# Eight block sums at the end of each up stage, on GpSimd in place of VectorE

## The chip, the cores and the metric

The kernel runs on one core of one Trainium2 chip. The metric is the device time of one execution in microseconds (us). The kernel before was timed three times: 1130.04, 1131.62 and 1132.43 us, median 1131.62 us.

Engine names are those of the profile: PE is TensorE's matmul stream and PEld its weight loads, DVE is VectorE, ACT is ScalarE, POOL is GpSimd, SP is the engine whose queue issues nearly all transfers (SPq). SBUF is the memory on the chip that all engines read, PSUM the one that PE writes its sums to.

## The reference

The reference is an attention followed by two feed-forward stages. What matters here are the two stages; in numpy, on 1792 tokens of 768 features:

```python
def _moe_ref(x, w_in, w_out):                 # d_ff = 2048
    h = np.maximum(x @ w_in, 0.0)
    return (h * h @ w_out).astype(np.float32)

def _moe2_ref(x, w_gate, w_val, w_out):       # d_ff = 1536
    g = x @ w_gate
    silu = g * (1.0 / (1.0 + np.exp(-g)))
    val = x @ w_val
    return (silu * val @ w_out).astype(np.float32)
```

Each stage is an up product (into the hidden features), an elementwise function, and a down product (back to 768 features).

## The kernel before

**Seven products for eight.** Each matrix product is cut into two by two blocks and done by a scheme with seven block products (P1 to P7) in place of eight. Its operands are blocks and sums of blocks: of the hidden result, the blocks B11, B12, B21, B22 and four differences of them, T1 = B12 - B11, T3 = B22 - B12, T2 = B22 - T1, T4 = B21 - T2. The down product reads B21, T1, B22, B11, T2, T3 and T4, in that order (`DOWN`, `DUSE`).

**Splitting for precision.** PE multiplies in a format that is shorter than fp32. Every operand is therefore split in two: a high part, made on ACT by a cast, and a low part, made on DVE by a subtraction (value minus high part). Three matmuls take the place of one: high by high, high by low, low by high. PE can't begin a step before both parts of its operands are there. For the hidden blocks the split is `cleave` (L1303 for the high part on ACT, the low part on DVE through `tt`, L1102, written to `xat` in the first stage and to `xab` in the second); for the weights it is L516 on ACT and L271 on DVE, into the five buffers `ring`.

**Loops and order.** An up stage runs over groups of 2 x 128 hidden features: eight groups in the first stage (`ph` 0), six in the second, where each has a gate and a value part. Within a group come the seven products, each for the two halves of the tokens (`tp` 0 and 1); a matmul has 448 columns. One `step` is one product for one half: nine matmuls. `after` evicts a result from PSUM, by ACT (L1105) or with an addition on DVE (L1102, `xacc<-ps,xacc`). When the blocks of a group are complete, `put` enters the T sums into a list with a due time, counted in steps, and `run_sums` issues them through `sum_of`: on DVE, two inputs and one output of 128x448 in SBUF (L1102, `xacc<-xacc`). A finished block is sent to DRAM by SP two to five steps later (`hid<-xacc`, L1059), and comes back for the down product (`dn<-hid`, L1281) with both halves side by side. Each group has eight such sums, four for each half.

The down product is `down`: seven products of `ng` steps each (eight in the first stage, six in the second), 18 matmuls a step. Step n needs the two parts of the n-th hidden block (`cleave(n, 0)` and `cleave(n, 1)`) and of the n-th weight block. The order of the instructions on each engine is fixed by the program. `cleave(n + 2, 1)` is issued in step n before `run_sums` of the same step. For the last group, the sums fall due as follows: T1 of half 0 in the last step of the up stage, between the low parts of down step 0 and of down step 1; T3 of half 0 and T1 of half 1 in down step 0; T2, T3, T2 and T4 in down step 1; the last T4 in down step 2. Block B21 of the last group isn't sent through DRAM but split straight from where it lies.

POOL works in the attention only, adding probabilities (L783), normalising (L698) and scaling the result (L848); after 274 us it has no instruction left. SP's queue takes its transfers in order: the sends of the T sums, the loads of hidden blocks and of weights stand in one line.

The diff touches one line of `sum_of` (L1073).

Of the kernel before, what the change touches and what calls it, by code (L numbers as in the profile page):

```python
# [13 lines left out]
ALU = mybir.AluOpType  # L14
# [5 lines left out]
def kernel(  # L20
# [14 lines left out]
    nc = tc.nc  # L35
# [16 lines left out]
    NF = (DFF // P, DFF2 // P)  # L52
# [19 lines left out]
    def slot(s):  # L72
        return xacc[:, s * S:(s + 1) * S]
# [931 lines left out]
    def moe():  # L1005
# [38 lines left out]
        def run_sums():  # L1044
            now = [d for d in sums_due if d[0] <= clock["n"]]
            sums_due[:] = [d for d in sums_due if d[0] > clock["n"]]
            for _, args in now:
                sum_of(*args)
# [15 lines left out]
        def drop(m, name):  # L1064
            m["left"][name] -= 1
            if not m["left"][name]:
                free.append(m[name])

        def sum_of(ph, g, tp, name):
            m = parts[ph, g, tp]  # L1070
            a, b = {"T1": ("B12", "B11"), "T3": ("B22", "B12"), "T2": ("B22", "T1"), "T4": ("B21", "T2")}[name]
            m[name] = m["B12"] if name == "T3" else take()
            tt(nc.vector, slot(m[name]), slot(m[a]), slot(m[b]), ALU.subtract)  # L1073
            for x in (a, b):
                if x != "B12":
                    drop(m, x)
# [24 lines left out]
        def tt(eng, o, a, b, op=ALU.add):  # L1101
            eng.tensor_tensor(out=o, in0=a, in1=b, op=op)  # L1102
# [43 lines left out]
        def take():  # L1146
            return free.pop(0)
# [315 lines left out]
```

## Time and profile before

| what | value |
|---|---|
| median of three timed runs | 1131.62 us |
| profiled execution, its time | 1129.42 us |
| its span, first to last instruction | 1127.6 us |
| PE busy | 1112.9 us, 99% of the span |
| DVE busy | 872.0 us, 77% |
| ACT busy | 637.1 us, 56% |
| POOL busy | 211.8 us, 19%, all of it in the first quarter |
| granted TensorE clock | full, 1.000 on average |
| up stage 1, down stage 1, up stage 2, down stage 2 | from about 251, 457, 667 and 970 us |

Times within the trace count from the first instruction. In a timeline row stand the start, the time, the engine, the line, the operation, output and inputs, how many like it follow one another, and in brackets the idle time of the engine before it with what ended that. Rows of several merged instructions give the time from the first start to the last end; instructions of DVE overlap a little at their ends, so a pair of two 0.62 us sums is listed with 1.15 us. A line can be that of a helper: L1102 is every two-input operation that goes through `tt`, so the output and the inputs tell which it is.

### The profile page before, as it was taken

The numbers are of one execution on the slowest core, as the hardware profiler recorded it, in microseconds if no ns is written. First come the engines' busy times: TensorE is split into PE (matmuls) and PEld (weight loads), VectorE is DVE, ScalarE is ACT, GpSimd is POOL, SyncE is SP. The second block draws the span as 40 slices with busy tenths as digits, with TensorE's granted clock in tenths as the row PEclk, the third lists the DMA queues.
The fourth block names the chain that finished last, engine by engine and source line by source line (L and its number), as shares of the span: only waits on it lengthen the run. The fifth ranks groups of instructions, "written<-read, shape, count | busy, mean of one in ns | idle before, by whom it ended". The sixth has DMA issues, their size and how long they took to land.

```text
span 1127.6 us, 17076 instructions
## 1 busy us (share of the span) xinstructions
PE 1112.9 (99%) x6164; PEld 946.4 (84%) x6164; DVE 872.0 (77%) x1255; ACT 637.1 (56%) x1049; POOL 211.8 (19%) x220
## 2 busy tenths in 40 slices
PE   7999999999999999999999999999999999999998
PEld 5556655559989999899999999999999999999997
DVE  7778888769897887898657788979787885875554
ACT  6887887665876676755544545443443534355332
POOL 5899899742000000000000000000000000000000
PEclk9999999999999999999999999999999999999999
DMA  6444333110798987965544402756464651874552
GB/s 166 129 115 126 99 98 82 46 35 18 238 299 273 296 288 255 346 234 184 184 130 119 127 1 79 246 165 192 142 209 141 224 173 68 309 257 125 180 164 98
DMA packets 115812, 187.76 MB, mean 167 GB/s; under 512 B 13840, under 2 KB 97040, under 8 KB 115728
## 3 DMA queue, kind: packets, MB, share of 16 engines
q1 hardware_dynamic: 115408, 186.68, 51.7%
q8 instruction: 48, 0.79, 0.3%
q14 instruction: 36, 0.29, 0.1%
q10 hardware_dynamic: 320, 0.00, 0.0%
HBM read 128.19 MB, written 58.28 MB: 165 GB/s over the span
## 4 chain that ended last, share of the span: by engine, by line
PE 89%; DMA 3%; DVE 3%; ACT 2%; issue 1%; SPq 0%; POOL 0%; DVEq 0%; ACTq 0%; POOLq 0%
PE ps L1140 41%; PE ps L1345 30%; PE s L792 6%; PE s L777 6%; PE s L748 2%; PE s L716 2%; PE s L813 2%; ACT xacc L1105 1%; DMA dn<-wkeep 1%; DVE xacc L1102 1%; PE s L757 1%; DMA raw<-in_k_dram 1%; DMA xacc<-in_moe_w_in_dram 1%; DVE mxz L751 0%; DVE conv L268 0%
## 5 line engine op out<-in xcount | busy, mean ns | idle before, releaser
L1140 PE MATMUL ps<-xb,ring 128*128 128x448 f32 x1080 | 225.6, 365 | 1.3 <-ACT xacc L1105 1.3
L1140 PEld LDWEIGHTS ps<-xb,ring 128*128 128x128 f32 x1080 | 202.8, 188 | 17.7 <-ACT xacc L1105 1.7
L1345 PE MATMUL ps<-xat,ring 128*128 128x448 f32 x1008 | 205.2, 366 | 1.3 <-DVE xat L1102 1.3
L1345 PEld LDWEIGHTS ps<-xat,ring 128*128 128x128 f32 x1008 | 189.1, 188 | 17.3 <-DVE xat L1102 2.3
L1140 PE MATMUL ps<-xat,ring 128*128 128x448 f32 x720 | 155.5, 365 | 0.0
L1345 PE MATMUL ps<-xab,ring 128*128 128x448 f32 x756 | 153.7, 365 | 0.2 <-DVE xab L1102 0.2
L1345 PEld LDWEIGHTS ps<-xab,ring 128*128 128x128 f32 x756 | 141.9, 188 | 11.9 <-DVE xab L1102 0.6
L1140 PEld LDWEIGHTS ps<-xat,ring 128*128 128x128 f32 x720 | 135.2, 188 | 10.7
L1105 ACT ACTIVATE xacc<-ps 128x448 f32<-128x448 f32 x148 | 79.0, 543 | 94.8 <-PE ps L1140 86.6
L1102 DVE TENSOR_TENSOR xacc<-ps,xacc 128x448 f32<-128x448 f32 x164 | 100.1, 620 | 34.3 <-PE ps L1140 20.7
L268 DVE SCALAR_TENSOR_TENSOR conv<-xacc,conv 128x768 int32<-128x768 int32 x124 | 119.7, 965 | 3.6
L1105 ACT ACTIVATE xacc<-xacc 128x448 f32<-128x448 f32 x148 | 85.0, 577 | 65.8 <-DVE xacc L1102 62.9
L1140 PE MATMUL ps<-xab,ring 128*128 128x448 f32 x540 | 116.2, 365 | 0.0
L751 DVE TENSOR_REDUCE mxz<-s 112x2 f32<-112x896 f32 x96 | 100.4, 1089 | 16.9 <-PE s L748 16.7
L1140 PEld LDWEIGHTS ps<-xab,ring 128*128 128x128 f32 x540 | 101.3, 188 | 8.7 <-issue 0.7
L1303 ACT CAST xat<-dn 128x896 fp32r<-128x896 f32 x55 | 51.9, 943 | 94.2 <-PE ps L1345 61.5
L271 DVE TENSOR_TENSOR ring<-conv,ring 128x384 fp32r<-128x384 f32 x127 | 70.7, 567 | 41.6 <-ACT ring L516 41.5
L779 ACT ACTIVATE p<-s 112x896 f32<-112x896 f32 x96 | 87.8, 920 | 20.8 <-PE s L777 16.1
L783 POOL TENSOR_TENSOR sg<-p 112x896 f32<-112x896 f32 x46 | 96.9, 2108 | 14.3 <-ACT p L779 14.3
L1102 DVE TENSOR_TENSOR xacc<-xacc 128x448 f32<-128x448 f32 x148 | 88.2, 618 | 1.1
L1102 DVE TENSOR_TENSOR xat<-dn,xat 128x896 fp32r<-128x896 f32 x55 | 59.9, 1088 | 34.2 <-ACT xat L1303 34.0
L1303 ACT CAST xab<-dn 128x896 fp32r<-128x896 f32 x41 | 38.7, 945 | 76.1 <-PE ps L1345 57.8
(101 smaller groups left out, 1363.9 us busy)
## 6 DMA issues: line engine op xcount, KB each, us to landing
hid<-xacc SPq DMA_DIRECT2D x192, 224.0 KB
dn<-hid SPq DMA_DIRECT2D x96, 448.0 KB
xacc<-in_moe_w_out_dram SPq DMA_DIRECT2D x28, 768.0 KB
xacc<-in_moe_w_in_dram SPq DMA_DIRECT2D x16, 768.0 KB
xacc<-in_moe_w_gate_dram SPq DMA_DIRECT2D x12, 768.0 KB
xacc<-in_moe_w_val_dram SPq DMA_DIRECT2D x12, 768.0 KB
wkeep<-conv SPq DMA_DIRECT2D x22, 384.0 KB
dn<-wkeep SPq DMA_DIRECT2D x44, 192.0 KB
```

The lines of the kernel that those rows point to most:

```text
L268: nc.vector.scalar_tensor_tensor(out=out, in0=in0, scalar=scalar, in1=out, op0=op, op1=ALU.bitwise_or)
L271: nc.vector.tensor_tensor(out=out, in0=a, in1=b, op=ALU.subtract)
L751: nc.vector.tensor_reduce(out=mxz[:, c, 0:P:D], in_=ps[:CP, :, :S], op=ALU.max, axis=AX.X)
L777: nc.tensor.matmul(ps[:CP, a, :S], lhs, rhs, start=(w == 0), stop=(w == 3))
L779: nc.scalar.activation(out=p, in_=ps[:CP, :, :S], func=AF.Exp)
L783: nc.gpsimd.tensor_tensor(out=sg, in0=p_t[pi, 2 * w], in1=p_t[pi, 2 * w + 1], op=ALU.add)
L792: nc.tensor.matmul(ps[s, :S], v_t[pi][:, a, c * D:(c + 1) * D], p[:, a, :], start=(c == 0), stop=(c == NCH - 1),)
L1102: eng.tensor_tensor(out=o, in0=a, in1=b, op=op)
L1105: nc.scalar.activation(out=slot(s), in_=src, func=func)
L1140: nc.tensor.matmul(ps, w[:, wi, kk * P:(kk + 1) * P], xk[:, xi, kk * S:(kk + 1) * S], start=bool(first and mm == 0), stop=(mm == 3 * KT - ...
L1303: nc.scalar.copy(k[:, 0], src)
L1345: nc.tensor.matmul(ps_of(ps[tp, o]), w[:, wi, o * P:(o + 1) * P], h[:, hi, tp * S:(tp + 1) * S], start=bool(first and m == 0), stop=(g == ...
```

## The change

`sum_of` chooses the engine: for the last group of each stage (`g == NF[ph] // 2 - 1`: g = 7 in the first stage, g = 5 in the second) the difference is issued on POOL, for all other groups on DVE as before. Eight sums of each stage, 16 in all, are concerned. Order of issue, buffers, due times and transfers are the same.

```diff
             m = parts[ph, g, tp]
             a, b = {"T1": ("B12", "B11"), "T3": ("B22", "B12"), "T2": ("B22", "T1"), "T4": ("B21", "T2")}[name]
             m[name] = m["B12"] if name == "T3" else take()
-            tt(nc.vector, slot(m[name]), slot(m[a]), slot(m[b]), ALU.subtract)
+            eng = nc.gpsimd if g == NF[ph] // 2 - 1 else nc.vector
+            tt(eng, slot(m[name]), slot(m[a]), slot(m[b]), ALU.subtract)
             for x in (a, b):
```

## Rows read from the trace of the kernel before

**Rows 1.** The page, part 1: span, then busy time and share of each engine.
```profile
span 1127.6 us, 17076 instructions
PE 1112.9 (99%) x6164; PEld 946.4 (84%) x6164; DVE 872.0 (77%) x1255; ACT 637.1 (56%) x1049; POOL 211.8 (19%) x220
```

**Rows 2.** Timeline of PE, start of down stage 1.
```profile
457.36 11.31 PE L1345 MATMUL ps<-xat,ring 128*128 128x448 f32 x55
469.44 3.98 PE L1345 MATMUL ps<-xat,ring 128*128 128x448 f32 x18 [0.78 <-DVE xat L1102]
473.93 16.24 PE L1345 MATMUL ps<-xat,ring 128*128 128x448 f32 x78 [0.50 <-DVE xat L1102]
```

**Rows 3.** Timeline of PE, start of down stage 2.
```profile
970.12 4.02 PE L1345 MATMUL ps<-xab,ring 128*128 128x448 f32 x19
974.37 25.80 PE L1345 MATMUL ps<-xab,ring 128*128 128x448 f32 x126 [0.23 <-DVE xab L1102]
```

**Rows 4.** Timeline of DVE, same stretch of stage 1.
```profile
453.91 0.62 DVE L1102 TENSOR_TENSOR xacc<-ps,xacc 128x448 f32<-128x448 f32 x1 [1.20 <-PE ps L1140]
...
455.75 1.09 DVE L1102 TENSOR_TENSOR xat<-dn,xat 128x896 fp32r<-128x896 f32 x1 [0.75 <-ACT xat L1303]
...
459.23 0.61 DVE L1102 TENSOR_TENSOR xacc<-xacc 128x448 f32<-128x448 f32 x1
...
465.77 1.15 DVE L1102 TENSOR_TENSOR xacc<-xacc 128x448 f32<-128x448 f32 x2
...
468.30 1.09 DVE L1102 TENSOR_TENSOR xat<-dn,xat 128x896 fp32r<-128x896 f32 x1
...
469.77 2.23 DVE L1102 TENSOR_TENSOR xacc<-xacc 128x448 f32<-128x448 f32 x4
...
472.79 1.08 DVE L1102 TENSOR_TENSOR xat<-dn,xat 128x896 fp32r<-128x896 f32 x1
```

**Rows 5.** Busy time by window: PE, PEld, DVE, ACT, POOL; clock, DMA share, GB/s.
```profile
454.00:462.00 8.00, 8.00 (x41) 7.42 (x40) 5.38 (x9) 7.46 (x14) 0.00 (x0) 1.00 1.04 383
462.00:476.00 14.00, 12.72 (x61) 11.07 (x61) 13.90 (x22) 7.60 (x12) 0.00 (x0) 1.00 1.00 357
967.30:973.20 5.90, 5.90 (x31) 5.43 (x30) 4.69 (x8) 3.24 (x5) 0.00 (x0) 1.00 1.01 365
```

**Rows 6.** Timeline of DVE, start of down stage 2.
```profile
972.70 0.62 DVE L1102 TENSOR_TENSOR xacc<-xacc 128x448 f32<-128x448 f32 x1
973.23 1.09 DVE L1102 TENSOR_TENSOR xab<-dn,xab 128x896 fp32r<-128x896 f32 x1
```

**Rows 7.** Timeline of ACT: the last two operations that make B12 of half 0.
```profile
452.74 1.19 ACT L1105 ACTIVATE xacc<-xacc 128x448 f32<-128x448 f32 x2 [0.63 <-DVE xacc L1102]
```

**Rows 8.** Groups by line and shape, whole span: busy us, mean ns; idle, releasers.
```profile
L118 DVE TENSOR_TENSOR xab<-xacc,xab 128x448 fp32r<-128x448 f32 x9 | 7.7, 856 | 0.0
L731 DVE TENSOR_TENSOR th<-s,th 128x448 fp32r<-128x448 f32 x24 | 15.0, 623 | 15.4 <-ACT th L724 15.0
L271 DVE TENSOR_TENSOR dn<-dn 128x384 f32<-128x384 f32 x34 | 18.9, 555 | 0.7
```

**Rows 9.** Timeline of POOL, three instructions late in the attention and after it.
```profile
119.01 2.66 POOL L698 TENSOR_TENSOR qk<-raw,r 112x512 f32<-112x512 f32 x1
...
262.38 1.21 POOL L848 TENSOR_TENSOR xacc<-xu,rb 128x448 f32<-128x448 f32 x1 [4.94 <-DMA rb<-row]
272.03 1.53 POOL L848 TENSOR_TENSOR xacc<-xu,rb 128x448 f32<-128x448 f32 x1 [8.44 <-DMA rb<-row]
```

**Rows 10.** Timeline of DVE beside those.
```profile
119.29 0.61 DVE L118 TENSOR_TENSOR xab<-xacc,xab 128x448 fp32r<-128x448 f32 x1
119.82 0.95 DVE L268 SCALAR_TENSOR_TENSOR conv<-xacc,conv 128x768 int32<-128x768 int32 x1
...
262.59 1.41 DVE L271 TENSOR_TENSOR conv<-conv 128x384 f32<-128x384 f32 x1
...
272.44 1.53 DVE L271 TENSOR_TENSOR ring<-conv,ring 128x384 fp32r<-128x384 f32 x1
```

## The prediction

> **What bounds the kernel now.** The page's busy times come first: PE is busy for 1112.9 of 1127.6 us, 99% [rows 1]. So the place of the change matters only where PE waits, and the second view is PE's timeline at the two places where the last group's sums are made, the starts of the down stages. There PE waits three times, each time for a low part that DVE makes: 0.78 and 0.50 us in stage 1 [rows 2], 0.23 us in stage 2 [rows 3]. That is 1.51 us in all, and the most that any relief of DVE at these places can give back. The third view is DVE's timeline [rows 4]: the sums of the last group are the x1 at 459.23, the x2 at 465.77, the x4 at 469.77 (an eighth follows after 474), and the low parts that PE waits for are the 128x896 rows at 468.30 and 472.79, behind these sums. The windows say how full DVE is: 13.90 of 14 us from 462 to 476, but only 5.38 of 8 us just before [rows 5]. Down step 0 begins at 457.36, and 55 matmuls take 11.31 us, so a step of 18 takes 3.7 us [rows 2].
>
> **What the change removes.** Eight DVE sums in each stage. One costs 0.61 us alone; two in a row take 1.15 and four 2.23 us [rows 4], so 0.54 us a sum from start to start. In stage 1 three of them stand before the low part of step 3 (459.23 and the pair), which gives 1.6 us, and four more before that of step 4: 2.15 us. In stage 2 one stands before the low part of step 1 (972.70, then 973.23 [rows 6]): 0.5 us.
>
> **What it adds.** Eight POOL instructions in each stage, of two SBUF inputs, 128x448. The nearest row is the scaling of the attention (L848), same shape, also two SBUF inputs: 1.21 us where nothing holds it up [rows 9]. POOL is free, and 8 x 1.21 is under 10 us, so POOL as an engine is not the bound: no down step reads one of them before step 15 (stage 1) or step 11 (stage 2), where the last group's T1 is the operand. The sums have no program order with DVE any more. The first can start when B12 is there, at 452.74 + 1.19 = 453.93 [rows 7], 5.3 us before DVE did it; the others follow as soon as their inputs are there. So all eight come in one bunch, in the first 12 us or so after 453.9, among the low parts of steps 0 to 2.
>
> **What a POOL instruction does to DVE beside it.** The trace of before has both engines active at once only in the attention and just after it. At 262.59 a DVE subtraction of two SBUF inputs, 0.555 us by its group [rows 8], took 1.41 us while POOL ran its 1.21 us one from 262.38; at 272.44 another took 1.53 us, and the POOL instruction that had come at 272.03, while DVE was still busy, was itself drawn out to 1.53 us [rows 9, 10]. One waited for the other, in turn. DVE lost 1.41 - 0.555 = 0.86 and 1.53 - 0.555 = 0.98 us, mean 0.92 us for each POOL instruction. A DVE instruction that reads PSUM does not pay: L731, in the midst of POOL's work, has a mean of 0.623 us, while L118 of the same size, with two SBUF inputs, has a mean of 0.856 [rows 8] where it takes 0.61 unhindered [rows 10]. Nearly everything that DVE does at the start of a down stage has two SBUF inputs: both kinds of low parts, the sums, the weights' two-input conversions.
>
> So a sum that cost DVE 0.54 us now costs it 0.92 us wherever DVE has no pause, and nothing where it has one. Bounds for one sum: zero (no collision, or DVE goes first each time) and POOL's whole 1.21. I take 0.92, from the rows of the same shape and the same two engines.
>
> **The sum, stage 1.** Low part of step 3, now done at 468.30 + 1.09 = 469.39. Eight POOL sums lie before it: + 8 x 0.92 = 7.36. DVE's pauses that they fill: 8 - 5.38 = 2.62 us from 454 to 462 [rows 5]; besides, DVE's instruction at 453.91 reads PSUM [rows 4], and half a us of the first sum runs beside it: - 0.5. The three removed DVE sums: - 1.6. It ends at 472.0, 2.6 us later, and PE, which already waits there, waits 2.6 us more. Part of that wait is seen earlier, at step 1, whose low part is pushed too; it is the same delay and not added. The next wait of before (0.50 us, step 4) goes: its low part comes at 473.87 + 2.6 - 2.15 = 474.3, PE gets there at about 475.5. Stage 1: + 2.6 - 0.5 = + 2.1 us.
>
> **Stage 2.** Here DVE also makes the last elementwise products, and has pauses of 5.90 - 4.69 = 1.21 us between 967.3 and 973.2 [rows 5]. The first POOL sum runs beside a PSUM read. Five more, one behind each of the next five DVE instructions with two SBUF inputs, come before the low part of step 1, which is now done at 973.23 + 1.09 = 974.32 [rows 6]: + 5 x 0.92 - 1.21 - 0.54 = + 2.85, so 977.2. PE already waits for it (resumed at 974.37 [rows 3]), so + 2.8 us. The last two sums delay the low part of step 2 to about 980.5; PE wants it at 977.2 + 3.7 = 980.9, just covered.
>
> Together + 4.9 us: 4.1 with 0.86 for a collision, 5.7 with 0.98. The profiled execution has 1129.42 us (span 1127.6 and 1.8 around it), which gives 1134.3; it lies 2.2 us under the median of the runs, 1131.62, and on that base I forecast **1136.5 us**. The rest I cost at nothing: the sends of the sums find them done earlier than before (the last at about 466 in place of 475), so SP waits less for them; PSUM evictions of the first down product come 15 us and more later, long after POOL's last read. If the sums are not early, this cover is gone; that is the third case.
>
> **The rivals.** *No collision that counts* (the other side): POOL gets its turn only when DVE has a pause. For it speaks the row at 119.01: a POOL instruction was drawn out to 2.66 us while two DVE instructions in a row, 0.61 and 0.95 us, went through undisturbed [rows 9, 10]. Against it speak the two rows of the shape in question. Then PE's waits of 0.78, 0.50 and 0.23 us go, - 1.5 us, against which stands a first collision or two in each stage's pauses, up to + 1: about 1130.8 us. It decides from the point where a POOL sum costs DVE less than about 0.54 us on the mean (13 x 0.54 = 7.0 = the pauses, removed sums and ended waits of the two sums above), just what DVE's own sum cost.
>
> *Late sums hold SP's queue.* If POOL is kept waiting until DVE pauses after 476, the sends of the last sums wait at the head of SP's queue, and the hidden blocks and weights of the next steps stand behind them. For it: DVE has 0.1 us of pause in 14 [rows 5]. Against: it needs DVE to win each time, where the rows of the same shape show turns. Price: sums that were done by 472 to 475 come 4 to 6 us later, PE's slack of about 1 us for the steps behind is eaten, + 4 a stage: about 1139.6 us.
>
> *The whole row blocks.* A DVE instruction that comes just as POOL starts could lose POOL's whole 1.21 us; the two rows show 0.86 and 0.98, but they are two. With the 13 collisions counted (eight and five) that is 13 x (1.21 - 0.92) = 3.8 us more, 1140.3 us. This is the rule of the Trainium skill (SBUF — State Buffer, section "Who interferes with whom"): a DVE instruction with two SBUF inputs and a GpSimd instruction that reads SBUF exclude each other, the later one blocked until the first has ended. That they exclude each other the trace confirms; the length it shows is shorter.
>
> **How the numbers follow.** The forecast has 0.57, no collision 0.28, the held queue 0.10, the whole row 0.05. The measurement can tell about 0.2%, 2.3 us. The forecast's own range, from 4.1 to 5.7 with an error of 2 us in the pauses counted, lies above + 2.3 in nine cases of ten; the held queue and the whole row are slower; no collision lies within 2.3 us but for noise, since the waits hold only 1.5 us. Slower: 0.9 x 0.57 + 0.15 = 0.66; faster 0.05; same 0.29. The range takes in the middle of no collision and the held queue: 1130.5 to 1140. The forecast's own is 1134 to 1138.5.
>
> **What would show it.** POOL with 16 more instructions, eight from about 454 and eight from about 966, each 1.2 to 2.1 us long; DVE rows of 0.55 us stretched to about 1.4 beside them; low parts of steps 1 to 3 in stage 1 and 0 to 2 in stage 2 later than now, with PE waits of about 3 us in each stage, named for the same DVE rows. Wrong, if DVE's rows there keep their length, if PE's waits shrink, or if the waits are for transfers.

## The result, and the profile after

Timed against each other, the kernel before has a median of 1131.16 us and the changed one 1136.78 us, 20 runs each; the ratio is 1.0057, 95% interval 1.004 to 1.0075 (an estimate over the runs; the quotient of the medians is 1.0050). All ratios leave out the few executions in a slower state, such as two of 2834 and 3904 us further down. The change makes the kernel slower by 0.4 to 0.75%. In a second comparison (12 runs against 35) it was 1136.73 against 1132.61 us, ratio 1.0042, interval 1.0005 to 1.0078.

The profile after is of an execution of 1148.39 us, one of the longest of the 20. It holds all that the change does, and two things more that have to be kept apart from it. The page, part 1, and the new group of POOL (mean of one in ns behind the busy time):

```profile
span 1146.3 us, 17094 instructions
PE 1125.5 (98%) x6164; PEld 947.0 (83%) x6164; DVE 878.8 (77%) x1239; ACT 637.3 (56%) x1049; POOL 238.8 (21%) x236
...
L1103 POOL TENSOR_TENSOR xacc<-xacc 128x448 f32<-128x448 f32 x16 | 24.7, 1574 | 693.3 <-DVE xacc L1103 512.5
```

POOL has the 16 instructions more, DVE 16 fewer, and yet DVE is busy for longer than before, 878.8 against 872.0 us [rows 1]. A POOL sum takes 1.57 us on the mean, not the 1.21 of the unhindered row [rows 9].

PE's timeline at the start of the down stages answers to [rows 2] and [rows 3]. The helper and the down matmuls have moved down by one line (L1103, L1346):

```profile
460.86 4.15 PE L1346 MATMUL ps<-xat,ring 128*128 128x448 f32 x19
465.93 7.70 PE L1346 MATMUL ps<-xat,ring 128*128 128x448 f32 x36 [0.93 <-DVE xat L1103]
475.69 34.64 PE L1346 MATMUL ps<-xat,ring 128*128 128x448 f32 x159 [2.06 <-DVE xat L1103]
...
986.74 0.37 PE L1346 MATMUL ps<-xab,ring 128*128 128x448 f32 x1
987.95 3.92 PE L1346 MATMUL ps<-xab,ring 128*128 128x448 f32 x18 [0.85 <-DVE xab L1103]
992.78 17.49 PE L1346 MATMUL ps<-xab,ring 128*128 128x448 f32 x85 [0.91 <-DVE xab L1103]
```

A down step has 18 matmuls. The first of them multiplies two high parts, so it goes ahead of the step's low part: the 19 are step 0 and one more, and the wait of 2.06 us is for the low part of step 3.

PE's waits there are 2.99 us in stage 1 (1.28 before) and 1.76 us in stage 2 (0.23 before), all for low parts on DVE. Then DVE and POOL in stage 1, which answer to [rows 4]:

```profile
457.95 1.14 DVE L271 TENSOR_TENSOR ring<-dn,ring 128x384 fp32r<-128x384 f32 x1
459.24 1.81 DVE L1103 TENSOR_TENSOR xat<-dn,xat 128x896 fp32r<-128x896 f32 x1 [0.16 <-ACT xat L1304]
461.77 2.14 DVE L271 TENSOR_TENSOR ring<-dn,ring 128x384 fp32r<-128x384 f32 x2 [0.72 <-ACT ring L516]
463.83 2.04 DVE L1103 TENSOR_TENSOR xat<-dn,xat 128x896 fp32r<-128x896 f32 x1
465.80 1.51 DVE L271 TENSOR_TENSOR ring<-dn,ring 128x384 fp32r<-128x384 f32 x1
467.23 2.05 DVE L1103 TENSOR_TENSOR xat<-dn,xat 128x896 fp32r<-128x896 f32 x1
469.21 1.50 DVE L271 TENSOR_TENSOR ring<-dn,ring 128x384 fp32r<-128x384 f32 x1
470.63 0.55 DVE L297 TENSOR_SCALAR dn<-dn 128x768 int32<-128x768 int32 x1
...
474.55 1.08 DVE L1103 TENSOR_TENSOR xat<-dn,xat 128x896 fp32r<-128x896 f32 x1
```
```profile
457.51 2.59 POOL L1103 TENSOR_TENSOR xacc<-xacc 128x448 f32<-128x448 f32 x2 [180.42 <-ACT xacc L1106]
460.37 9.92 POOL L1103 TENSOR_TENSOR xacc<-xacc 128x448 f32<-128x448 f32 x6 [0.27 <-ACT xacc L1106]
```

While POOL works (457.5 to 470.3), every DVE row with two SBUF inputs is stretched: the first ones by less (1.14 instead of 0.55 us, 1.81 instead of 1.09), those from 463.83 on to 1.51 instead of 0.55 and 2.05 instead of 1.09. Once POOL is done, at 470.3, the rows that begin have their old length (L297 with 0.55). The low part of step 3 ends at 475.63, 14.77 us after the start of the down stage, against 12.03 before (469.39 after 457.36).

The third part is PE's clock. Windows of 1 us of the same execution (PE, PEld, DVE, ACT, POOL busy; then the granted clock):

```profile
475.00:476.00 1.00, 0.31 (x2) 0.30 (x3) 1.00 (x2) 1.00 (x2) 0.00 (x0) 1.00 0.91 321
476.00:477.00 1.00, 1.00 (x4) 0.91 (x3) 1.00 (x3) 0.33 (x1) 0.00 (x0) 0.53 0.96 361
477.00:478.00 1.00, 1.00 (x4) 0.87 (x4) 1.00 (x2) 0.00 (x0) 0.00 (x0) 0.50 0.97 285
478.00:479.00 1.00, 1.00 (x4) 0.87 (x4) 1.00 (x3) 0.00 (x0) 0.00 (x0) 0.50 0.92 276
479.00:480.00 1.00, 1.00 (x6) 0.91 (x5) 1.00 (x2) 0.00 (x0) 0.00 (x0) 0.76 0.96 357
480.00:481.00 1.00, 1.00 (x6) 0.92 (x5) 1.00 (x2) 0.00 (x0) 0.00 (x0) 1.00 1.03 391
```

PE had stood still for 2.06 us, went on, and from 476.0 to about 479.5 had the lower of its two levels (0.50, 1.2 in place of 2.4 GHz): 0.47 + 0.50 + 0.50 + 0.24 = 1.7 us lost. Before, with waits of 0.78 and 0.50 us, the clock stayed at 1.00 [rows 5]. Of the 18.7 us that this execution is longer, 13.3 are no work of the change: 3.5 us lie ahead of down stage 1, and 9.8 us (525.88 from down 1 to down 2, against 516.07 in a second profile, below) are a slow pace of the matmuls, told of at the end. What is left is 3.3 us from down 1 to down 2 and 2.1 us after it.

### The profile page after: what moved, and what is told of

The parts are those of the page before. It is cut to its first block, busy times and chain, and to the rows that moved or that the text cites. A ratio compares the mean times of both kernels' runs of the same rounds, so it can differ in the third digit from the quotient of the medians.

```text
span 1146.3 us, 17094 instructions
## 1 busy us (share of the span) xinstructions
PE 1125.5 (98%) x6164; PEld 947.0 (83%) x6164; DVE 878.8 (77%) x1239; ACT 637.3 (56%) x1049; POOL 238.8 (21%) x236
## 4 chain that ended last, share of the span: by engine, by line
PE 85%; DVE 5%; DMA 4%; issue 3%; ACT 2%; POOL 1%; SPq 1%; DVEq 0%; POOLq 0%; ACTq 0%
PE ps L1141 41%; PE ps L1346 30%; PE s L777 4%; PE s L792 4%; PE s L748 2%; PE s L716 1%; PE s L813 1%; DMA xacc<-in_moe_w_in_dram 1%; DVE mxz L751 1%; DVE ring L271 1%; DMA dn<-wkeep 1%; DVE xacc L1103 1%; POOL sg L783 1%; POOL qk L698 1%; DMA raw<-in_k_dram 1%
## 5 line engine op out<-in xcount | busy, mean ns | idle before, releaser
L1141 PE MATMUL ps<-xb,ring 128*128 128x448 f32 x1080 | 228.2, 367 | 1.3 <-ACT xacc L1106 1.3
L1346 PE MATMUL ps<-xat,ring 128*128 128x448 f32 x1008 | 210.6, 370 | 3.0 <-DVE xat L1103 3.0
L1346 PEld LDWEIGHTS ps<-xat,ring 128*128 128x128 f32 x1008 | 190.3, 189 | 23.1 <-DVE xat L1103 4.0
L1103 POOL TENSOR_TENSOR xacc<-xacc 128x448 f32<-128x448 f32 x16 | 24.7, 1574 | 693.3 <-DVE xacc L1103 512.5
L1141 PE MATMUL ps<-xat,ring 128*128 128x448 f32 x720 | 157.2, 367 | 0.0
L1346 PE MATMUL ps<-xab,ring 128*128 128x448 f32 x756 | 153.9, 365 | 1.8 <-DVE xab L1103 1.8
L1346 PEld LDWEIGHTS ps<-xab,ring 128*128 128x128 f32 x756 | 141.9, 188 | 13.7 <-DVE xab L1103 2.5
L1103 DVE TENSOR_TENSOR xacc<-ps,xacc 128x448 f32<-128x448 f32 x164 | 100.3, 620 | 37.8 <-PE ps L1141 24.0
L268 DVE SCALAR_TENSOR_TENSOR conv<-xacc,conv 128x768 int32<-128x768 int32 x124 | 122.7, 990 | 3.6
L1103 DVE TENSOR_TENSOR xat<-dn,xat 128x896 fp32r<-128x896 f32 x55 | 62.5, 1137 | 38.5 <-ACT xat L1304 38.5
```

The costliest lines, as they stand in the source:

```text
L268: nc.vector.scalar_tensor_tensor(out=out, in0=in0, scalar=scalar, in1=out, op0=op, op1=ALU.bitwise_or)
L1141: nc.tensor.matmul(ps, w[:, wi, kk * P:(kk + 1) * P], xk[:, xi, kk * S:(kk + 1) * S], start=bool(first and mm == 0), stop=(mm == 3 * KT - ...
L1346: nc.tensor.matmul(ps_of(ps[tp, o]), w[:, wi, o * P:(o + 1) * P], h[:, hi, tp * S:(tp + 1) * S], start=bool(first and m == 0), stop=(g == ...
```

## The experiments

Since single executions differ by such things, each profile is cut at PE's first down matmuls of the two stages. All numbers are us, from PE's timelines and the spans:

| kernel | from down 1 to down 2 | from down 2 to the end |
|---|---|---|
| before; before, second profile | 512.76; 512.53 | 157.48; 159.97 |
| changed, first profile (slow pace); second profile | 525.88; 516.07 | 159.56; 159.59 |
| stage 1 only | 514.38 | 157.34 |
| stage 2 only | 512.68 | 159.37 |
| sums left out | 511.04 | 156.97 |
| POOL writes only | 510.72 | 157.97 |
| POOL twice | 522.45 | 160.21 |
| late sums on DVE; second profile (slow pace) | 510.72; 520.58 | 157.05; 156.99 |
| late sums on POOL; one copy a step | 515.53; 513.94 | 158.60; 158.23 |

The theory: a POOL instruction that reads SBUF and a DVE instruction with two SBUF inputs exclude each other, in strict turns; DVE's low parts come late by that, and PE waits for them. Rivals: another cause on PE (pace), POOL's activity as such, transfers behind late sums, or one stage alone.

**The changed kernel again.**

> The changed kernel once more, timed and with a second profile. Theory of the port (each GpSimd sum holds up one VectorE instruction with two SBUF inputs by 0.9 to 1.0 us, the low parts of steps 1 and 3 of down stage 1 and of steps 0 and 1 of down stage 2 come late, PE waits, and after the longest wait its clock falls for some us): + 4 to + 6 us against the kernel before; PE waits of 2.7 to 3.3 us at the start of down stage 1 and 1.5 to 2.0 us at that of down stage 2, named for the low part on VectorE. Rival, the pace (what costs time is that matmuls after a wait follow one another at 207 in place of 203 ns over hundreds of us, as in the first profile of the changed kernel, from 466 to 987): 98 or 99 matmuls in 20 us instead of 100 or 101 from 480 to 980 in this profile too. If this profile shows 100 or 101 there and the time is still + 4 to + 6, the pace is an accident of single executions.

Ratio 1.0042 (1.0005 to 1.0078). PE's waits were 0.85 and 2.20 us in stage 1, 0.92 and 0.91 in stage 2. The clock again, behind the wait of 2.20 us:

```profile
472.97 9.32 PE L1346 MATMUL ps<-xat,ring 128*128 128x448 f32 x37 [2.20 <-DVE xat L1103]
```
```profile
472.00:474.00 2.00, 1.03 (x3) 0.94 (x4) 2.00 (x3) 1.25 (x2) 0.00 (x0) 0.74 0.94 323
474.00:476.00 2.00, 2.00 (x7) 1.78 (x6) 2.00 (x4) 0.00 (x0) 0.00 (x0) 0.50 0.92 273
```

From 480 on there were 100 or 101 matmuls in 20 us (890 from 480 to 660, as before), so the slow pace is not needed for the loss: this execution took 1135.92 us without it.

**One stage at a time.**

```diff
-            eng = nc.gpsimd if g == NF[ph] // 2 - 1 else nc.vector
+            eng = nc.gpsimd if ph == 0 and g == NF[ph] // 2 - 1 else nc.vector
```

This is the kernel with stage 1 only; the one with stage 2 only has `ph == 1` there.

> Only the eight sums of the first stage go to GpSimd, those of the second stay on VectorE. Theory of the port: + 3 to + 4.5 us (PE's waits at the start of down stage 1 from 1.3 to about 3.0 us, and about 1.7 us for some 3.5 us at half the clock after a wait of 2 us), and down stage 2 as in the kernel before (one wait of 0.2 us). Rival, one stage carries it all: + 5.6 or 0.

> Only the eight sums of the second stage go to GpSimd. Theory of the port: + 1.5 to + 2 us, PE's waits at the start of down stage 2 from 0.2 to about 1.8 us, no fall of the clock, since no wait is longer than 1 us; stage 1 with its waits of 0.8 and 0.5 us as before. My prediction had + 2.8 for this stage and + 2.1 for the first, so by its sizes this one would be the larger.

Medians 1134.92 and 1133.96 us beside 1132.61 of before; the ratios, 1.0013 (0.9978 to 1.0048) and 1.0017 (0.9988 to 1.0047), don't tell either from no change. The profiles do: + 1.7 us from down 1 to down 2 with stage 1 alone (514.38 against 512.65, the mean of the two of before) and nothing afterwards; + 1.9 us after down 2 with stage 2 alone (159.37 against 157.48) and nothing ahead of it. The 159.97 of the second profile of before is no base for this piece: it holds matmuls at a slow pace, 485 between 1000 and 1100 us, where the first profile has 495 and the stage-2 kernel 496. In the stage-1 kernel PE waited as long as in the changed one, and the clock did not fall:

```profile
476.49 5.73 PE L1346 MATMUL ps<-xat,ring 128*128 128x448 f32 x27 [2.17 <-DVE xat L1103]
```
```profile
476.00:478.00 2.00, 1.51 (x7) 1.42 (x8) 2.00 (x4) 0.00 (x0) 0.00 (x0) 1.00 0.92 280
```

So in these profiles stage 1 costs 1.7 us with the clock up, and 516.07 - 512.65 = 3.4 us with its fall. Of the 20 timed runs of the changed kernel 17 have a mean clock of 0.998 or 0.999, three of 1.000. In the comparison of the two stages 12 of the 35 runs of the kernel before lie under 1.000 too, and a mean doesn't tell where the clock fell: that the fall at this place is the common case is likely, not shown. I expected 3 to 4.5 us for stage 1 and had taken the fall for certain.

**The sums left out.**

```diff
-            tt(nc.vector, slot(m[name]), slot(m[a]), slot(m[b]), ALU.subtract)
+            if g != NF[ph] // 2 - 1:
+                tt(nc.vector, slot(m[name]), slot(m[a]), slot(m[b]), ALU.subtract)
```

> The eight block sums of the last group of each stage are left out altogether, on VectorE and on GpSimd; transfers and order stay. Relief of VectorE alone: PE's three waits of 0.78, 0.50 and 0.23 us go, - 1.0 to - 1.5 us. So taking the sums off VectorE is worth at most this, and the rest of the way to the changed kernel, 6 to 7 us, is the price of GpSimd's work. Rival, VectorE's relief is worth nothing since ScalarE or a transfer is late next: 0 +- 0.5 and PE waits at the same steps with another name.

Median 1129.65 us, ratio 0.9995 (0.9962 to 1.0027): the times don't tell it from no change. In the profile PE has no wait left at either place; the row runs through from the first down matmul of stage 1:

```profile
457.39 42.85 PE L1346 MATMUL ps<-xat,ring 128*128 128x448 f32 x209
```

- 1.6 and - 0.5 us in the two pieces. So by this profile the relief of DVE is there, and it is worth 2.1 us, somewhat more than the 1.0 to 1.5 expected; what POOL's work costs on top is 516.07 - 511.04 and 159.59 - 156.97, together 7.7 us (1.7 of it the clock).

**POOL writes, without reading.** The subtraction is replaced by `nc.gpsimd.memset(slot(m[name]), 0.0)`.

> GpSimd writes zeros into the eight blocks of the last group instead of subtracting (the sums themselves are left out): the same number of GpSimd instructions at the same place, but without a read of SBUF. Theory of the port, with the reads as what collides: VectorE's instructions beside them keep their 0.55 and 1.09 us, PE has no wait at either place, and the time is that of the kernel without the sums, - 1 to - 3 us against before. Rival, any GpSimd instruction that touches SBUF holds up VectorE: VectorE's rows stretched beside the writes by about the length of a write, and PE's waits at least as long as before (+ 0 to + 4 us).

Median 1130.81 us, ratio 0.9998 (0.9974 to 1.0022), no change told where I had - 1 to - 3 us. Seven of POOL's eight writes in each stage stand at the place of the sums, 0.43 us each (the first lies 7 to 11 us ahead); the DVE rows beside them have their old lengths, here two of stage 2:

```profile
968.13 1.72 POOL L1076 MEMSET xacc<- 128x448 f32 x4 [0.53 <-DVE xacc L1105]
```
```profile
967.99 0.55 DVE L271 TENSOR_TENSOR ring<-dn,ring 128x384 fp32r<-128x384 f32 x1
...
969.15 1.08 DVE L1105 TENSOR_TENSOR xab<-dn,xab 128x896 fp32r<-128x896 f32 x1
```

No wait of PE in stage 1; one of 0.46 us in stage 2, where I had none (for a low part behind a DVE pause of 1.86 us that waited on ACT). So it is not POOL's activity as such that collides; what the writes lack, and the sums have, are the reads.

**POOL twice.**

```diff
             tt(eng, slot(m[name]), slot(m[a]), slot(m[b]), ALU.subtract)
+            if g == NF[ph] // 2 - 1 and name != "T3":
+                tt(eng, slot(m[name]), slot(m[a]), slot(m[b]), ALU.subtract)
```

> GpSimd makes six of its eight sums twice in a row (all but the one done in place), 14 instructions in each stage. Theory of the port with strict turns (behind each VectorE instruction with two SBUF inputs one GpSimd instruction gets in): in down stage 1 there are 14 such VectorE instructions up to the low part of step 3, of which 8 were held up and now 13 or 14 are, so that low part comes 5 to 6 us later than in the changed kernel and PE's waits there sum to 8 to 9 us instead of 3; in down stage 2 the low part of step 1 has no more such instructions ahead of it than before, so PE's waits stay at 1.8 us (at most + 0.5 at steps 2 and 3, where a low part every 3.4 us is still faster than a step of 3.7). Together + 5 to + 8 us on the changed kernel, nearly all of it in stage 1. Rival, without turns (delay goes with GpSimd's work): both stages get + 5 to + 6 us. Rival, GpSimd only gets in when VectorE pauses: + 0 to + 1.

PE's waits are 0.92 and 7.47 us in stage 1, and 0.92, 0.91 and 0.39 us in stage 2:

```profile
480.34 19.97 PE L1348 MATMUL ps<-xat,ring 128*128 128x448 f32 x84 [7.47 <-DVE xat L1105]
...
988.80 11.21 PE L1348 MATMUL ps<-xab,ring 128*128 128x448 f32 x54 [0.91 <-DVE xab L1105]
1000.40 19.93 PE L1348 MATMUL ps<-xab,ring 128*128 128x448 f32 x97 [0.39 <-DVE xab L1105]
```

8.4 and 2.2 us: both as the strict turns have it, and as neither rival has it. In DVE's rows each instruction up to the low part of step 3 is stretched, L297 too, which has a single tensor as input:

```profile
470.01 1.51 DVE L297 TENSOR_SCALAR dn<-dn 128x768 int32<-128x768 int32 x1
471.55 3.59 DVE L268 SCALAR_TENSOR_TENSOR dn<-xacc,dn 128x768 int32<-128x768 int32 x2
...
478.27 2.01 DVE L1105 TENSOR_TENSOR xat<-dn,xat 128x896 fp32r<-128x896 f32 x1
480.21 0.55 DVE L271 TENSOR_TENSOR ring<-dn,ring 128x384 fp32r<-128x384 f32 x1
```

The time missed: median 1152.39 us, 19.3 us above the 1133.08 of the kernel before in the same comparison, ratio 1.0166 (1.0133 to 1.02). That is some 14 us more than the changed kernel's + 4.1 and + 5.6, where I had 5 to 8. The profiled execution, the shortest of its six, has a span of 1142.9 us, 9.1 above the changed kernel's second. In it the clock is at 0.50 from about 476 to 486; half of the 5.7 us in which PE worked by then is 2.8 us. With 7.1 us more of waits than before this makes 9.9 us, and the piece from down 1 to down 2 is 522.45 - 512.65 = 9.8 us longer. Why the median is longer still I can't show; the mean clock, 0.995 in this shortest run and 0.995 to 0.997 in the others, doesn't explain it.

**Late sums on DVE and on POOL.** In `put` the due times of the last group move by three down steps (stage 1) and one (stage 2); a down step is two counts. The sends follow the sums after two counts in place of four.

```diff
-            for new, needs, wait in (("T1", ("B11", "B12"), 1 + end), ("T3", ("B22", "T1"), 2),
+            for new, needs, wait in (("T1", ("B11", "B12"), 1 + end + (6, 2)[ph] * end), ("T3", ("B22", "T1"), 2),
...
-                    sends_due.append((t + 3 + end, (ph, g, tp, new)))
+                    sends_due.append((t + 3 - end, (ph, g, tp, new)))
```

> The sums stay on VectorE, but those of the last group are issued three down steps later in stage 1 and one step later in stage 2, behind the low parts that PE waits for; their sends follow two counts after them. If what the sums cost before was only their place in VectorE's order, PE's waits of 0.78, 0.50 and 0.23 us go as in the kernel without the sums: - 1.0 to - 2.0 us against before, and it beats both kernels. Rival: the low parts of steps 5 to 8 become late in their place, or a hidden block behind the later sends: PE waits there of 0.5 to 1.5 us and no gain.

> The late sums on VectorE once more, to narrow the interval: ratio to the kernel before 0.998 to 0.999 (- 1.0 to - 2.0 us) if the three waits of PE are gone for good, no PE wait at either place in the profile.

No wait of PE at either place, in both profiles; - 1.9 and - 0.4 us in the two pieces of the first (- 1.6 and - 0.5 without any sums). The times don't settle it: ratios 0.9994 (0.9969 to 1.002) and 1.0006 (0.9974 to 1.0037). Both lie under the changed kernel's 1.0057 and 1.0042; that it beats the kernel before, by some 0.2%, only the pieces of the first profile say. The second holds the slow pace (520.58 from down 1 to down 2), so its first piece can't be compared.

On POOL with the same due times, each sum behind a copy of 8 columns of the newest low part:

> The sums are on GpSimd as in the changed kernel, but ahead of each a GpSimd copy of 8 columns of the newest low part keeps it from starting before that low part is done; the due times are those of the kernel with late sums on VectorE (three steps later in stage 1, one in stage 2). Theory of the port: each sum still holds up one VectorE instruction by 0.9 to 1.0 us, but now the low parts of steps 5 to 8 in stage 1, which have 2 to 3 us to spare: PE's waits in stage 1 fall from 3.0 to under 1 us and the time from + 5 to between - 1 and + 2 us. Stage 2 has the sums behind the low part of step 2 and following, with 2 us and more to spare: its waits fall from 1.8 to under 0.5. Rival, GpSimd's sums cost the same wherever they stand (they finish late, or the sends behind them are late): + 4 to + 6 as in the changed kernel.

> The late sums on GpSimd once more, since their first profile was of a disturbed execution and shows nothing; the first runs lay 2 to 12 us above the kernel before, against the - 1 to + 2 expected. What the profile decides: if the low parts of steps 5 to 8 are late (VectorE's rows there stretched by 0.9 to 1.0 us beside the sums and shorter beside the 8-column copies), the theory of the port holds and the spare time was smaller than I took it; PE then waits 2 to 5 us in one of these steps for VectorE. If PE's waits are under 1 us, the time is lost elsewhere (a transfer behind the late sends, or PE's pace or clock).

> As the late sums on GpSimd, but one copy of 8 columns ahead of the first sum of each step instead of one ahead of each sum: four or five small GpSimd instructions fewer in each stage. Theory of the port with turns: each small copy also takes one turn and holds up one VectorE instruction by its length (0.2 to 0.4 us, estimated from the 16- and 32-column rows of the attention, 0.21 to 0.25 us), so this one is 0 to 2 us faster than the kernel with eight copies. Rival: no difference.

The first profile has a span of 3902 us and shows nothing of the change. Ratios 1.0054 (1.0027 to 1.0081), 1.004 (1.0015 to 1.0064) and, with fewer copies, 1.0052 (1.0019 to 1.0086): no gain on the changed kernel. My expectation of - 1 to + 2 fell in stage 1. The profile with a copy ahead of each sum:

```profile
492.20 18.05 PE L1350 MATMUL ps<-xat,ring 128*128 128x448 f32 x80 [2.38 <-DVE xat L1105]
```
```profile
484.20 2.12 DVE L1105 TENSOR_TENSOR xat<-xacc,xat 128x448 fp32r<-128x448 f32 x2
486.25 1.51 DVE L271 TENSOR_TENSOR ring<-conv,ring 128x384 fp32r<-128x384 f32 x1
487.79 1.55 DVE L274 TENSOR_TENSOR conv<-dn 128x384 f32<-128x384 f32 x1
...
490.13 2.01 DVE L1105 TENSOR_TENSOR xat<-dn,xat 128x896 fp32r<-128x896 f32 x1
```

The collisions are the same, 0.96 us at 486.25, and now it is the low part of step 8 that is late (145 matmuls ran ahead of the wait, eight steps of 18). DVE has no pause there either, so the spare time of the steps was used up one after another. With one copy a step the waits are 1.06 and 1.34 us at steps 7 and 8. In stage 2, where DVE has pauses, the waits for DVE are gone, as expected; the one wait of PE left there is 0.17 us and for an eviction by ACT. Whether the copies themselves cost time the runs don't tell apart.

**The kernel before again.**

> The kernel before against itself: ratio 1 within its interval, which says what the other ratios are worth. In its profile PE's waits at the two places should be 1.3 and 0.2 us again, without a fall of the clock there. If matmuls at 207 ns show up in some stretch here too, the slow pace is no work of the change.

Ratio 0.9988 (0.9958 to 1.0018): a comparison of 12 runs can be 0.1% off without any cause. PE's waits were 0.55 and 0.57 us in stage 1 and none in stage 2. The piece after down 2 is 2.5 us longer than in the first profile; matmuls came at the slow pace for a part of it, as said above.

## Why the prediction was right, point by point

*POOL is free and its sums come early, in a bunch*: right. The first started 3.4 us ahead of the down stage, the eighth was done 9.4 us after its start (470.29 after 460.86); DVE had its seventh done 14.6 us after it (472.00 after 457.36 [rows 2, 4]). No wait for a transfer took the sums' place, so the held queue is out.

*One collision costs 0.92 us*: measured 1.51 - 0.55 = 0.96 us, and 0.95 to 0.96 in each of the four rows from 463.83 on, where one POOL sum follows each DVE instruction. The low part of step 0, where a PSUM read and a pause lie ahead, lost 0.7. The rival in which DVE goes first did not happen once at the down stages; why it did at 119.01 [rows 9, 10] no run here shows. "The whole row" would have been 1.21. The Trainium skill (SBUF — State Buffer, section "Who interferes with whom") also has it that a GpSimd instruction that only writes SBUF does not contend with a DVE instruction of two SBUF inputs. The kernel with writes agrees, with 0.55 and 1.08 us.

*Stage 1, low part of step 3 later by 2.6 us*: measured 14.77 - 12.03 = 2.74. That it fits so well is luck, since two terms of the sum were too large and go against each other. The stretches add up to 0.59 + 0.72 + 1.11 + 0.95 + 0.96 + 0.96 + 0.95 = 6.24 us, where the sum has 7.36 - 0.5 = 6.86: only the later ones cost their full 0.96. And the POOL sums did not fill all of DVE's pauses. Before, these were 0.75 [rows 4] and the two in the following rows of before, 2.5 us in all; 0.16 + 0.72 = 0.9 us of pauses are left after, so 1.6 us were filled, not 2.62. With the 1.6 us of the removed sums that makes 3.0, by rows that overlap a little at their ends, for the 2.74.

```profile
458.29 1.03 DVE L271 TENSOR_TENSOR ring<-dn,ring 128x384 fp32r<-128x384 f32 x2 [1.44 <-ACT ring L516]
...
461.84 1.09 DVE L1102 TENSOR_TENSOR xat<-dn,xat 128x896 fp32r<-128x896 f32 x1 [0.28 <-ACT xat L1303]
```

*The next wait goes*: right. Net + 2.1 forecast, + 1.7 measured where the clock stays up. That PE's clock falls after the longer wait was no term of my sum: + 1.7 us in both profiles of the changed kernel.

*Stage 2, + 2.8 us*: over-sized, + 1.9 and + 2.1 measured, with PE waits of 1.76 us where I had named about 3. The term at fault is the five full collisions ahead of the low part of step 1. The rows of after:

```profile
984.42 1.52 DVE L271 TENSOR_TENSOR ring<-dn,ring 128x384 fp32r<-128x384 f32 x1
985.86 0.61 DVE L1103 TENSOR_TENSOR xacc<-ps,xacc 128x448 f32<-128x448 f32 x1
986.39 1.50 DVE L1103 TENSOR_TENSOR xab<-dn,xab 128x896 fp32r<-128x896 f32 x1
987.82 2.93 DVE L271 TENSOR_TENSOR ring<-dn,ring 128x384 fp32r<-128x384 f32 x2
990.68 0.61 DVE L1103 TENSOR_TENSOR xacc<-ps,xacc 128x448 f32<-128x448 f32 x1
991.21 1.52 DVE L1103 TENSOR_TENSOR xab<-dn,xab 128x896 fp32r<-128x896 f32 x1
```

Both low parts stand behind an eviction that reads PSUM, 0.61 us as ever, and POOL's next sum ran half beside it: the low parts lost only 1.50 - 1.09 and 1.52 - 1.09, 0.4 us each. The stretches add up to 0.97 + 0.41 + 1.9 + 0.43 = 3.7 us instead of 4.6. I had counted this for the first sum and not for these.

Together: 1.7 + 1.7 + 1.9 to 2.1, some 5.4 us by the pieces of executions in which the clock falls, against 4.9 forecast and 5.6 measured between the medians (4.1 in the second comparison). The mechanism was right; that the sum fits this well comes of misses that cancel, the clock (not seen) and stage 2 (too large).

## What to carry to other kernels

Work taken off a busy engine helps only if what takes it over does not stop the first one: here a sum that cost DVE 0.54 us in its own queue cost it 0.96 us from POOL's, at each place where DVE had no pause and read two SBUF operands. Before moving an elementwise operation to POOL, count the DVE instructions that stand beside it with two SBUF inputs, and find the PE step that waits for the last of them. Those that read PSUM kept their 0.61 us here; a row with a single SBUF tensor (L297) did not keep its 0.55 us, so one input alone is no safe sign. An order on the same engine that puts the sums behind what PE waits for (the late sums on DVE) removed the waits that the move was to remove, though the times don't tell this kernel from the one before.

## What the runs showed of the hardware that was not expected

**A fall of the clock after a short wait.** After waits of 2.06, 2.20 and 2.38 us PE worked for some 3.4 us at the lower level, which cost 1.7 us; after 2.17 us in another execution it did not. With the wait of 7.47 us the fall lasted for 10 us, of which the first 4 still belong to the wait. After waits of 1.34 us and less no profile shows one at these places. What decides it at about 2 us stays open.

**Two paces of the same matmuls.** With the granted clock at 1.00, the matmuls of 448 columns follow one another either at 120/594 us = 202 ns or at 120/582 = 206 ns, for hundreds of us. The first row below is of the changed kernel, the second of the kernel before, the third of the kernel with late sums on DVE, which had no wait of PE in either down stage:

```profile
840.00:960.00 120.00, 120.00 (x582) 109.00 (x581) 96.87 (x160) 52.10 (x96) 0.00 (x0) 1.00 0.53 177
```
```profile
840.00:960.00 120.00, 120.00 (x594) 111.19 (x593) 89.91 (x149) 50.96 (x96) 0.00 (x0) 1.00 0.46 153
```
```profile
840.00:960.00 120.00, 120.00 (x582) 109.00 (x581) 93.04 (x155) 51.22 (x95) 0.00 (x0) 1.00 0.48 157
```

Over the 500 us from 480 to 980 that is 2%, 9 to 10 us. In the stage-1 kernel it held from 280 to 440 (771 matmuls instead of 784), ahead of anything that was changed. So it is no effect of the change, and it fits the scattered runs of 1138 to 1150 us that all kernels have, before included (1141.22). What starts and ends it stays open.
